# Wide matmuls on column groups for the feed-forward products and the shift vector, and folded modulation halves added on VectorE

## The chip, the cores and the metric

The kernel runs on one core of a Trainium2 chip. The metric is the device time of one execution in microseconds (us); the kernel before takes 594.23 us (median of three runs, 593.74 to 595.05). A core has five engines that follow their own instruction streams in order: PE (TensorE, matmuls; its weight loads are listed as PEld), DVE (VectorE), ACT (ScalarE), POOL (GpSimd) and SP (SyncE). Here POOL and SP do little but issue transfers (DMA), each into a queue of its own; 16 DMA engines carry both. SBUF is the on-chip memory of 128 partitions, PSUM the banks that matmuls write, DRAM the memory outside.

## What is computed

The reference is one transformer-like block, forward and backward, for a single token, in bfloat16. From a conditioning vector `c` it makes six vectors; shift, scale and gate for an attention part A, and shift, scale and gate for a feed-forward part B:

```python
mod = (_silu(c) @ w_mod).reshape(c.shape[0], 6, 1, -1)        # w_mod: 1024 x 6144
sa, ca, ga, sb, cb, gb = (mod[:, 0], ..., mod[:, 5])
h = _layernorm(x) * (1 + ca) + sa
x = x + ga * _A_ref(h, A_k_cache, A_v_cache, A_wq, A_wo)      # attention
h = _layernorm(x) * (1 + cb) + sb
x = x + gb * _B_ref(h, B_w_gate, B_w_up, B_w_down)            # sigmoid(h w_gate) * (h w_up), times w_down
```

A has 32 query heads of 128 and four key/value heads, and looks at the last 4096 of 65536 cached positions. B has 3584 hidden units. The outputs are the block's result and the gradients by every input: `x`, both caches (4 x 65536 x 128 each, zero outside the last 4096 positions), `wq`, `wo`, `w_gate`, `w_up`, `w_down`, `c` and `w_mod`. Weight gradients are outer products of two vectors, as large as the weights. The reference's own matmuls have one row, so all is bound by moving weights and gradients; the zeros of the two cache gradients alone are about 120 transfers of 1 MB.

## The kernel before

The order of the instructions on each engine is that of the source: the kernel is written under a manual schedule, so a position in the text is a position in the queue. Vectors of 1024 lie in columns: element `k*128 + p` on partition `p`, column `k`. A 1024x1024 weight is eight tiles of 128x1024 bf16.

A product of a vector with a weight is done in two ways. The *narrow* way (`mod_tiles`, `front`, `ffn_mm`) makes the weight the stationary operand and the vector column the moving one: one matmul gives one column of 128 results, already in column layout. The *wide* way (`rows_mm`, L432 to 438) makes the vector column, broadcast to 32 columns, the stationary operand and streams 32 columns of each of the weight's 128-column heads past it, in four column groups: group `a` writes partitions 32a to 32a+31. There every partition of a group holds the same row of results; `rows_to_cols` (L440 to 444) multiplies by `mask`, which is the identity repeated for the four groups, and sums 32 neighbours, on DVE, and so brings the row back into columns.

The work goes in stages, in the profile's times:

- 0 to 25 us: the tiles of the first two sections of `w_mod` (`wm01_t`) come in on SP's queue, loads of K, `wq` and V on POOL's. `mod_ps` is computed in the wide way (loop from L471), and the two sections of each tile are folded: the second half is multiplied by the broadcast layer norm `b1k` (`mulv`, L476, L489), and `w01_fold` (L453 to 469) transposes the sum of both halves into `w01_T`, as 16 matmuls with the identity into two fp32 banks, copied out by ACT ("A") or DVE ("V").
- 25 to 66: transposes of K and `wq`, queries, scores, softmax. At its end `rsum` (L590) is the reciprocal of the sums, and four zero fills wait for it on POOL.
- 68 to 155: products with V and the per-head work with `wo` (L709, `n_ps`).
- 155 to 305: `b_ps` (L766), 512 matmuls in units that other work is put between (`bch`); the other four sections of `w_mod` are loaded, multiplied and summed (`fold_sum`, L943). Here the shift vector `sb_` is made by `mod_tiles` (L384) in two halves, into `md_ps` (L954 to 983).
- 306 to 480: the feed-forward loop, seven blocks `q` of 512 hidden units. A block's tiles of `w_up` and `w_gate` come by `load_ug` (L936), `w_down` by `load_wd` (L924, SP). `front` (L1026) makes gate and up products, `gates` (L1037) the two sigmoids on ACT, `hh_ops` the hidden vector, `ffn_mm` (L1047) the product with `w_down`, which `ffn` sums over blocks. `wd_ttr` and `wd_outer` make the gradient of the hidden vector and of `w_down` (on DVE, lines 250 and 246), `dug_part` the gradient at gate and up, and the loop over `j` the gradient into `h2` and the outer products that are stored over the weights' tiles (`store_ug`, L942). `side()` puts in left-over transposes (L909, `tp_side`, copied by ACT at L910).
- 480 to 570: backward through attention. `op_ps` (L1160) rearranges the heads' outputs; then `dattn`, gradients of `wo`, V, `wq`, K and of the sections of `w_mod`.
- 570 to 592: only transfers.

Transfers of zeros are put at chosen places (`zero(n, after)`, lines 206, 200, 194, 191; in the feed-forward loop by the table `Z_FFN`), so that the queue always holds work. With `after`, or when a source tile isn't ready, POOL waits at its issue, and all that stands behind it on POOL waits too. PSUM banks come in rotation from `new_ps`, `new_tp` and `new_bank`/`new_acc`; the latter two share one bank, tag "acc", which `md_ps`, `fg` and `op_ps` use one after another.

Of the kernel before, what the change touches and what calls it, by code (L numbers as in the profile page):

```python
# [10 lines left out]
P = 128  # L11
# [48 lines left out]
def kernel(  # L60
# [157 lines left out]
    def new_ps(name="ps"):  # L218
        p, tag = next_pool()
        return p.tile([P, 512], FP32, name=name, tag=tag)  # L220
# [4 lines left out]
    def new_acc(name="acc"):  # L225
        return new_bank(name)[:, 0:64]
# [8 lines left out]
    def mulv(out, a, b):  # L235
        return tt(out, a, b, ALU.mult)

    def addv(out, a, b):
        return tt(out, a, b, ALU.add)

    def cp(out, a):
        return nc.vector.tensor_copy(out=out, in_=a)  # L242
# [138 lines left out]
        eng.dma_start(out=ar(off, 2 * n).rearrange("p (j x) -> p j x", j=n),  # L381
                            in_=wm_view[:, j:j + n, sct * D:(sct + 1) * D])

    def mod_tiles(ps, tiles, ts_, first, last=KD - 1):  # L384
        for t in ts_:
            for k in range(KD):
                nc.tensor.matmul(ps[:, k:k + 1], lhsT=tiles[t][:, k * P:(k + 1) * P],
                                 rhs=cs_bf[:, t:t + 1], start=(first and t == ts_[0] and k == 0), stop=(t == last),
                                 skip_group_check=True)

    def mod_rows(out, tiles):
        ps = new_bank("mod_rows")
# [45 lines left out]
        return mm  # L438

    def rows_to_cols(out, ps, n, room=scr):  # L440
        f = room.bitcast(FP32)[:, 0:32 * n].rearrange("p (n r) -> p n r", r=32)
        tt(f, ps[:, 0:32 * n].rearrange("p (n r) -> p n r", r=32),
           mask.rearrange("p (o r) -> p o r", o=1).broadcast_to([P, n, 32]), ALU.mult)
        nc.vector.reduce_sum(out=out, in_=f, axis=AX.X)
# [7 lines left out]

    def w01_fold(j, eng):  # L453
        cols = slice(j * P, (j + 1) * P)
        for k in range(2):
            ps = new_ps("w01_ps")
            for i in range(4):
                nb = 4 * k + i
                for sct in range(2):
                    c0 = sct * D + nb * P  # L460
                    nc.tensor.matmul(ps[:, i * P:(i + 1) * P], lhsT=wm01_t[j][:, c0:c0 + P], rhs=ident_bf[:, :],  # L461
                                     start=(i == 0 and sct == 0), stop=(sct == 1), skip_group_check=True)
            o = w01_T[:, 4 * k:4 * k + 4, cols]
            v = ps.rearrange("p (n m) -> p n m", n=4)
            if eng[k] == "A":
                nc.scalar.copy(out=o, in_=v)
            else:
                cp(o, v)

    rot[:] = [(psum, "mm"), (pna, "na"), (pgu, "gu"), (ppq, "pq"), (px, "x"), (pna, "na"), (prq, "rq")]  # L470
    mod_ps = new_bank("mod_ps")  # L471
    for j in range(KD):
        rows_mm(mod_ps, cs_bf[:, j:j + 1], heads(wm01_t[j]), j == 0, j == KD - 1)
        if j < KD - 1:
            mulv(wm01_t[j][:, D:2 * D], wm01_t[j][:, D:2 * D], b1k)
        if j > 1:  # L476
            w01_fold(j - 2, "AA")
    mod_col = vt([P, KM], "mod_col")
    rows_to_cols(mod_col[:, 0:16], mod_ps, 16)
    sa, ca, ga = mod_col[:, 0:8], mod_col[:, 8:16], mod_col[:, 16:24]  # L480
# [5 lines left out]
    addv(h1, h1, sa)  # L486
    h1_bf = vt([P, KD], "h1_bf", BF16)
    cp(h1_bf, h1)
    mulv(wm01_t[KD - 1][:, D:2 * D], wm01_t[KD - 1][:, D:2 * D], b1k)  # L489
    w01_fold(KD - 2, "AV")  # L490
    w01_fold(KD - 1, "AV")

    def kT_unit(i):
        g, tb = divmod(i, G)
# [456 lines left out]
    fold_T = [tr_unit(w2_t[t]) for t in range(KD)]  # L951

    h2 = vt([P, KD], "h2")
    md_ps = new_acc("md_ps")  # L954
    for t in range(4):
        fold_sum(t, (b1k, scr))
    bch(1)
    mod_tiles(md_ps, sb_t, range(4), True)
    bch(1)
    fold_T[0]()  # L960
    bch(1)
# [17 lines left out]
    wm_sec(5, 4, 1, 56, nc.sync)  # L979
    cp(scr, B_t[4])  # L980
    B_t[4] = scr
    mod_tiles(md_ps, sb_t, range(4, 8), False)
    cp(sb_, md_ps[:, 0:KD])
    mulv(h2, ln2, cb1)
    addv(h2, h2, sb_)
    h2_bf = vt([P, KD], "h2_bf", BF16)
# [1 line left out]
    for t in range(4, 8):  # L988
# [29 lines left out]
    small = [{k: vt([P, w], "%s%d" % (k, i), dt) for k, w, dt in  # L1018
              (("sg", 4, FP32), ("om", 4, FP32), ("dhh", 4, FP32), ("hh", 4, FP32), ("hh_bf", 4, BF16),
               ("hom", 4, FP32), ("dug_bf", 8, BF16))} for i in range(2)]  # L1020
    fg = new_acc("fg")
    ffn_ps = fg[:, 0:KD]
    ffn = vt([P, KD], "ffn")
    gu_t = [fg[:, 16 + 8 * i:24 + 8 * i] for i in range(2)]

    def front(q):  # L1026
        gu = gu_t[q % 2]
        for k in range(2):
            for j in range(KD):
                for i in range(4):  # L1030
                    f0 = 256 * (i // 2) + i % 2
                    col = 4 - 4 * k + i
                    nc.tensor.matmul(gu[:, col:col + 1], lhsT=ug_v[:, q % 2, j // 4, j % 4, k, f0:f0 + 255:2],  # L1033
                                     rhs=h2_bf[:, j:j + 1], start=(j == 0 and i == 0), stop=(j == KD - 1),
                                     skip_group_check=True)

    def gates(q):  # L1037
        r, gu = small[q % 2], gu_t[q % 2]
        nc.scalar.activation(out=r["sg"], in_=gu[:, 0:4], func=ACT.Sigmoid)
        nc.scalar.activation(out=r["om"], in_=gu[:, 0:4], func=ACT.Sigmoid, scale=-1.0)  # L1040

    def hh_ops(q):
        r, up = small[q % 2], gu_t[q % 2][:, 4:8]
        mulv(r["hh_bf"], r["sg"], up)
        mulv(r["hh"], r["sg"], up)
        mulv(r["hom"], r["hh"], r["om"])

    def ffn_mm(q, s):
        for i in (2 * s, 2 * s + 1):
            for k in range(KD):  # L1050
                nc.tensor.matmul(ffn_ps[:, k:k + 1], lhsT=wd_v[:, i, k * P:(k + 1) * P],  # L1051
                                 rhs=small[q % 2]["hh_bf"][:, i:i + 1], start=(i == 0 and k == 0),
                                 stop=(i == 3), skip_group_check=True)

    def wd_ttr(q, s):
        for i in (2 * s, 2 * s + 1):
# [42 lines left out]
    for q in range(NB):  # L1099
        z = Z_FFN[q]  # L1100
        more = q + 1 < NB
        for j in range(KD):
            w = ug_v[:, q % 2, j // 4, j % 4, :, :].rearrange("p k f -> p (k f)")
            ttr(w, w, dug_b, dh2acc[:, q * KD + j:q * KD + j + 1])
            if not more and j in (3, 5, 6):
                unpark({3: 2, 5: 0, 6: 4}[j])
            (outer_act if j < 5 else outer_dve)(w, h2[:, j:j + 1], dug_b)
            if more and j == 4:
                front(q + 1)
                gates(q + 1)  # L1110
            if more and (j > 4 or (j == 1 and q)):
                side()
            if j == 0:
                if q == 0:
                    cp(ffn, ffn_ps)
                else:
                    addv(ffn, ffn, ffn_ps)
            if j == 3:
                store_ug(q, 0, 4)
                zero(z[0])  # L1120
        store_ug(q, 4, 4)
        zero(z[1])
        if more:
            hh_ops(q + 1)
            ffn_mm(q + 1, 0)
            wd_ttr(q + 1, 0)
            wd_outer(q + 1, 0)
            ffn_mm(q + 1, 1)
            side(3 if q < 2 else 2)
            wd_ttr(q + 1, 1)  # L1130
            dug_part(q + 1)
            if q + 2 < NB:
                load_ug(q + 2, 0, 4)
            wd_outer(q + 1, 1)
            zero(z[2])
            side()
            if q + 2 < NB:
                load_ug(q + 2, 4, 4)
            zero(z[3])
            if q + 2 < NB:  # L1140
                load_wd(q + 2, 0)
                load_wd(q + 2, 1)
        else:
            zero(z[2] + z[3])
    assert not jobs
    for p in (1, 3):
        unpark(p)
    nc.scalar.copy(out=B_home[5], in_=B_t[5])
# [276 lines left out]
```

## Time and profile before

| | us |
|---|---|
| median of 3 runs | 594.23 (593.74 to 595.05) |
| profiled execution, its own time | 594.11 |
| its span | 592.3 |
| PE, PEld busy | 403.6, 256.7 |
| DVE, ACT, POOL busy | 364.3, 263.5, 156.4 |
| mean granted PE clock | 0.775 |
| bytes moved, mean rate | 246.57 MB, 416 GB/s |

The span runs from the first to the last recorded instruction or transfer of the profiled execution; its own time includes what lies around it. Busy times of different engines overlap. A row of a timeline or of the groups names the line, the engine, the operation, the tile that is written and read with its shape, and, in brackets, how long the engine was idle before it and which instruction ended that. Since most vector and copy work goes through helpers, several steps share a line: 233 is every elementwise product or sum of two tensors, 242 every copy on DVE, 246 a product with a per-partition scalar, 250 a product with a sum along the row, 436 every wide matmul. The tile names tell them apart; large tiles are views of one `arena`. The row of the granted clock gives 0.5 to 0.6 of full speed through most of the feed-forward loop.

### The profile page before, as it was taken

To read this page: it belongs to the slowest core of one execution; us is meant where nothing else is said; L and a number is where in the kernel's file an instruction comes from. 1 tells how busy PE (TensorE), PEld (TensorE's weight loads), DVE (VectorE), ACT (ScalarE), POOL (GpSimd) and SP (SyncE) were. 2 spreads that over 40 slices of the span, in tenths; PEclk is the share of its full clock that TensorE was granted. 3 is DMA by queue.
4 is the path that set the end of the run, shared out by engine and by line. 5 is a ranking of instruction groups with operands and counts; after the bars stand their busy time and mean duration, and the time that the engine had idled before them with its cause. 6 is when DMAs were issued, how large, how long until landed. Compare 5 with 4: busy or idle time off the path is not lost.

```text
span 592.3 us, 10137 instructions
## 1 busy us (share of the span) xinstructions
PE 403.6 (68%) x4107; PEld 256.7 (43%) x4132; DVE 364.3 (62%) x684; ACT 263.5 (44%) x401; POOL 156.4 (26%) x258
## 2 busy tenths in 40 slices
PE   3996689999999999978866236244363455977600
PEld 2784333334344546534436225244253335656500
DVE  3765499999511020176548686687866878778740
ACT  2589514567211014212135376464655645965400
POOL 3113123212223112222221334224343145113200
PEclk9999699999999999997995567555555558755555
DMA  8999999999999999999999999999999999999998
GB/s 349 420 420 420 413 454 392 464 421 430 425 422 397 432 452 419 433 431 400 413 422 395 419 413 413 411 411 416 415 414 413 418 419 408 416 426 420 414 419 360
DMA packets 37486, 246.57 MB, mean 416 GB/s; under 512 B 6097, under 2 KB 6097, under 8 KB 23712
## 3 DMA queue, kind: packets, MB, share of 16 engines
q0 software_dynamic: 30144, 218.65, 92.3%
q1 hardware_dynamic: 7248, 27.27, 12.7%
q8 instruction: 32, 0.52, 0.3%
q14 instruction: 14, 0.11, 0.1%
q10 hardware_dynamic: 48, 0.01, 0.0%
HBM read 78.28 MB, written 185.60 MB: 446 GB/s over the span
## 4 chain that ended last, share of the span: by engine, by line
PE 38%; DMA 23%; DVE 18%; issue 9%; ACT 6%; POOL 1%; ACTq 0%; DVEq 0%; POOLq 0%; SPq 0%
PE b_ps L766 17%; DMA out_dram<-arena 13%; DVE arena L233 6%; PE n_ps L709 6%; DMA arena<-in_B_w_down_dram 5%; DVE arena L250 5%; DMA arena<-in_B_w_gate_dram 4%; DVE arena L246 3%; ACT arena L519 2%; PE t_ps L667 2%; PE tp_side L909 1%; PE tp_k L498 1%; PE w_ps L461 1%; PE ok L629 1%; PE do L1189 1%
## 5 line engine op out<-in xcount | busy, mean ns | idle before, releaser
L766 PE MATMUL b_ps<-arena 128*128 128x512 bf16 x494 | 116.4, 384 | 2.5 <-ACT arena L910 1.1
L910 ACT COPY arena<-tp_side 128x1024 bf16<-128x1024 bf16 x62 | 60.9, 1015 | 71.2 <-PE tp_side L909 71.2
L233 DVE TENSOR_TENSOR arena<-arena 128x2048 bf16<-128x2048 bf16 x64 | 76.5, 1223 | 2.3 <-PE n_ps L709 0.3
L766 PEld LDWEIGHTS <-arena 128*128 128x128 bf16 x512 | 49.3, 99 | 59.0 <-issue 5.8
L250 DVE CUSTOM_DVE_ANT_0 arena<-arena,scr 128x1024 bf16<-128x1024 bf16 x56 | 66.2, 1221 | 9.3 <-ACT scr L1072 9.3
L709 PE MATMUL n_ps<-arena 128*128 128x512 bf16 x249 | 65.2, 378 | 6.2 <-DVE arena L233 4.2
L200 POOL DMA_DIRECT2D out_dram<-out_dram x68 | 33.6, 495 | 116.0 <-PE n_ps L709 37.5
L909 PE MATMUL tp_side<-ident_bf,arena 128*128 128x128 bf16 x496 | 53.9, 285 | 12.6 <-DVE arena L233 5.3
L909 PEld LDWEIGHTS <-arena 128*128 128x128 bf16 x496 | 46.0, 132 | 18.4 <-issue 9.8
L1033 PE MATMUL fg<-h_bf,arena 128*128 128x1 bf16 x448 | 15.6, 166 | 48.6 <-DMA arena<-in_B_w_up_dram 25.5
L709 PEld LDWEIGHTS <-arena 128*128 128x128 bf16 x256 | 24.6, 97 | 41.2 <-issue 15.8
L250 DVE CUSTOM_DVE_ANT_0 arena<-arena,b1k 128x1024 bf16<-128x1024 bf16 x24 | 28.4, 1221 | 20.5 <-PE fg L1051 20.5
L281 ACT ACTIVATE arena<-scr,h 128x1024 bf16<-128x1024 bf16 x35 | 38.5, 1143 | 2.7 <-DVE dh2acc L250 2.3
L206 POOL DMA_DIRECT2D out_dram<-zeros x45 | 25.1, 561 | 55.0 <-PE q_ps L436 14.0
L942 POOL DMA_DIRECT2D out_dram<-arena x28 | 22.1, 793 | 63.0 <-ACT arena L281 43.8
L1033 PEld LDWEIGHTS <-arena 128*128 128x128 bf16 x448 | 13.9, 104 | 51.2 <-DMA arena<-in_B_w_up_dram 31.2
L1253 ACT ACTIVATE arena<-ps_kv 128x512 bf16<-128x512 f32 x48 | 26.4, 618 | 21.6 <-PE ps_kv L1249 21.6
L669 ACT CAST arena<-t_ps 128x512 bf16<-128x512 f32 x56 | 30.1, 589 | 12.1 <-PE t_ps L667 12.1
L242 DVE CAST arena<-b_ps 128x512 bf16<-128x512 f32 x6 | 4.2, 692 | 50.8 <-PE b_ps L766 50.8
L1249 PE MATMUL ps_kv<-junk,arena 8*128 8x128 bf16 x256 | 28.7, 307 | 5.6 <-DVE arena L246 5.6
L1249 PEld LDWEIGHTS <-arena 8*128 8x128 bf16 x256 | 25.2, 141 | 9.9 <-issue 9.8
L519 ACT COPY arena<-tp_wq 128x1024 bf16<-128x1024 bf16 x23 | 21.4, 1070 | 7.3 <-PE tp_wq L517 7.3
(315 smaller groups left out, 634.3 us busy)
## 6 DMA issues: line engine op xcount, KB each, us to landing
out_dram<-zeros POOLq DMA_DIRECT2D x45, 1024.0 KB, 14.0
out_dram<-arena POOLq DMA_DIRECT2D x28, 1024.0 KB, 15.4
out_dram<-arena POOLq DMA_DIRECT2D x30, 512.0 KB, 11.5
out_dram<-arena SPq DMA_DIRECT2D x20, 512.0 KB, 10.4
arena<-in_A_wq_dram POOLq DMA_DIRECT2D x8, 1024.0 KB, 20.9
arena<-in_A_wo_dram POOLq DMA_DIRECT2D x8, 1024.0 KB, 12.4
arena<-in_w_mod_dram POOLq DMA_DIRECT2D x7, 1024.0 KB, 18.6
arena<-in_B_w_up_dram POOLq DMA_DIRECT2D x14, 512.0 KB, 12.0
```

What stands on the lines that cost most here:

```text
L200: ins = nc.gpsimd.dma_start(out=as_rows(region, BIGP).bitcast(FP32), in_=zero_src[:, 0:P * ZW // 4].rearrange("i (p x) -> (i p) x", p=BIGP ...
L233: return nc.vector.tensor_tensor(out=out, in0=a, in1=b, op=op)
L250: return nc.vector.tensor_tensor_reduce(out=out, in0=w, in1=b, scale=1.0, scalar=0.0, op0=ALU.mult, op1=ALU.add, accum_out=acc)
L281: return nc.scalar.activation(out=out, in_=b, func=ACT.Copy, scale=col)
L519: nc.scalar.copy(out=blk, in_=tp[:, :])
L669: nc.scalar.copy(out=o, in_=ps)
L709: mm = nc.tensor.matmul(nbank[k][:, :], lhsT=k_nat[:, g, t_ * DH:(t_ + 1) * DH], rhs=vp[:, t_ % 2, 4 * k:4 * k + 4, :].rearrange("p h d -> ...
L766: mm = nc.tensor.matmul(bbank[p][k][:, :], lhsT=a4[:, p, h, :], rhs=wo_t[u][:, a, k * 512:(k + 1) * 512], start=(i == 0 and a == 0), stop= ...
L909: nc.tensor.transpose(tp[:, i * P:(i + 1) * P], blk[:, i * P:(i + 1) * P], ident_bf[:, :])
L910: nc.scalar.copy(out=blk if dst is None else dst, in_=tp[:, :])
L1033: nc.tensor.matmul(gu[:, col:col + 1], lhsT=ug_v[:, q % 2, j // 4, j % 4, k, f0:f0 + 255:2], rhs=h2_bf[:, j:j + 1], start=(j == 0 and i == ...
L1249: nc.tensor.matmul(ps[:, t4 * DH:(t4 + 1) * DH], lhsT=rows[32 * g:32 * g + HG, t_ * P:(t_ + 1) * P], rhs=hd[32 * g:32 * g + HG, :], start= ...
```

## The change

Three products go from the narrow to the wide way: the shift vector, the gate and up products, and the product with `w_down`. In the feed-forward loop both share one PSUM bank, `fg`: 256 columns for gate and up, 256 for the result with `w_down`. Because parts of the bank are accumulated over different stretches, it is cleared by DVE and every matmul adds (`start=False`): once before the loop, and the gate and up part again after each `rows_to_cols`, which works in place in PSUM. The result of `w_down` is summed over all seven blocks in PSUM and brought into columns once, behind the loop, instead of one addition per block. `gates(q + 1)` is moved from the middle of the `j` loop to behind `store_ug` and `zero` at its end. The streamed operand of `front` reads every second element of the tile, as the narrow weight load did.

Separately, the two halves of a `wm01` tile are added on DVE (`addv`) after the product, and the fold is eight transposes into one bf16 tile and one copy, instead of 16 matmuls that add in PSUM and two copies.

No transfer is added, dropped or moved against the others of its queue.

```diff
-    def mod_tiles(ps, tiles, ts_, first, last=KD - 1):
+    def mod_tiles(ps, tiles, ts_):
         for t in ts_:
-            for k in range(KD):
-                nc.tensor.matmul(ps[:, k:k + 1], lhsT=tiles[t][:, k * P:(k + 1) * P],
-                                 rhs=cs_bf[:, t:t + 1], start=(first and t == ts_[0] and k == 0), stop=(t == last),
-                                 skip_group_check=True)
+            rows_mm(ps, cs_bf[:, t:t + 1], heads(tiles[t]), t == 0, t == KD - 1)
...
     def rows_to_cols(out, ps, n, room=scr):
-        f = room.bitcast(FP32)[:, 0:32 * n].rearrange("p (n r) -> p n r", r=32)
+        room = room if room is ps else room.bitcast(FP32)
+        f = room[:, 0:32 * n].rearrange("p (n r) -> p n r", r=32)
...
     def w01_fold(j, eng):
         cols = slice(j * P, (j + 1) * P)
-        for k in range(2):
-            ps = new_ps("w01_ps")
-            for i in range(4):
-                nb = 4 * k + i
-                for sct in range(2):
-                    c0 = sct * D + nb * P
-                    nc.tensor.matmul(ps[:, i * P:(i + 1) * P], lhsT=wm01_t[j][:, c0:c0 + P], rhs=ident_bf[:, :],
-                                     start=(i == 0 and sct == 0), stop=(sct == 1), skip_group_check=True)
...
+        tp = new_tp("tp_w01")
+        for nb in range(KD):
+            nc.tensor.transpose(tp[:, nb * P:(nb + 1) * P], wm01_t[j][:, nb * P:(nb + 1) * P], ident_bf[:, :])
...
+    def w01_sum(j):
+        w, v = wm01_t[j][:, 0:D], wm01_t[j][:, D:2 * D]
+        mulv(v, v, b1k)
+        addv(w, w, v)
...
         if j < KD - 1:
-            mulv(wm01_t[j][:, D:2 * D], wm01_t[j][:, D:2 * D], b1k)
+            w01_sum(j)
         if j > 1:
-            w01_fold(j - 2, "AA")
+            w01_fold(j - 2, "A")
...
-    mulv(wm01_t[KD - 1][:, D:2 * D], wm01_t[KD - 1][:, D:2 * D], b1k)
-    w01_fold(KD - 2, "AV")
-    w01_fold(KD - 1, "AV")
+    w01_sum(KD - 1)
+    w01_fold(KD - 2, "A")
+    w01_fold(KD - 1, "V")
...
-    md_ps = new_acc("md_ps")
+    md_ps = new_bank("md_ps")[:, 0:256]
...
-    cp(sb_, md_ps[:, 0:KD])
+    rows_to_cols(sb_, md_ps, KD, md_ps)
...
-    fg = new_acc("fg")
-    ffn_ps = fg[:, 0:KD]
+    fg = new_bank("fg")
+    nc.vector.memset(fg, 0.0)
+    gu_ps, ffn_ps = fg[:, 0:256], fg[:, 256:512]
     ffn = vt([P, KD], "ffn")
-    gu_t = [fg[:, 16 + 8 * i:24 + 8 * i] for i in range(2)]
+    gu_t = [gb_rest] * 2
+
+    def ffn_rows(out, col, w, stop):
+        for a in range(4):
+            nc.tensor.matmul(out[32 * a:32 * a + 32, :], lhsT=col.broadcast_to([P, 32]), rhs=w[..., 32 * a:32 * a + 32],
+                             start=False, stop=stop, tile_position=(0, 32 * a), skip_group_check=True)

     def front(q):
-        gu = gu_t[q % 2]
-        for k in range(2):
-            for j in range(KD):
-                for i in range(4):
-                    f0 = 256 * (i // 2) + i % 2
-                    col = 4 - 4 * k + i
-                    nc.tensor.matmul(gu[:, col:col + 1], lhsT=ug_v[:, q % 2, j // 4, j % 4, k, f0:f0 + 255:2],
-                                     rhs=h2_bf[:, j:j + 1], start=(j == 0 and i == 0), stop=(j == KD - 1),
-                                     skip_group_check=True)
+        for j in range(KD):
+            w = ug_v[:, q % 2, j // 4, j % 4, :, :].rearrange("p k (s r i) -> p (k s) i r", s=2, i=2)
+            ffn_rows(gu_ps, h2_bf[:, j:j + 1], w, j == KD - 1)

     def gates(q):
         r, gu = small[q % 2], gu_t[q % 2]
+        rows_to_cols(gu, gu_ps, 8, gu_ps)
+        nc.vector.memset(gu_ps, 0.0)
...
     def ffn_mm(q, s):
         for i in (2 * s, 2 * s + 1):
-            for k in range(KD):
-                nc.tensor.matmul(ffn_ps[:, k:k + 1], lhsT=wd_v[:, i, k * P:(k + 1) * P],
-                                 rhs=small[q % 2]["hh_bf"][:, i:i + 1], start=(i == 0 and k == 0),
-                                 stop=(i == 3), skip_group_check=True)
+            ffn_rows(ffn_ps, small[q % 2]["hh_bf"][:, i:i + 1], heads(wd_v[:, i, :]),
+                     q == NB - 1 and i == 3)
...
                 front(q + 1)
-                gates(q + 1)
             if more and (j > 4 or (j == 1 and q)):
                 side()
-            if j == 0:
-                if q == 0:
-                    cp(ffn, ffn_ps)
-                else:
-                    addv(ffn, ffn, ffn_ps)
...
         if more:
+            gates(q + 1)
             hh_ops(q + 1)
...
     assert not jobs
+    rows_to_cols(ffn, ffn_ps, KD, ffn_ps)
     for p in (1, 3):
         unpark(p)
```

## The prediction

> **What bounds the kernel now.** I read the head of the page first (busy time, slices), then windows at the edges of the span, then the timeline where the changed lines run, and last what POOL's queue waits for.
>
> The head of the page: engine, busy time, share of the span; then the slices.
>
> ```profile
> span 592.3 us, 10137 instructions
> PE 403.6 (68%) x4107; PEld 256.7 (43%) x4132; DVE 364.3 (62%) x684; ACT 263.5 (44%) x401; POOL 156.4 (26%) x258
> ...
> DMA  8999999999999999999999999999999999999998
> ...
> DMA packets 37486, 246.57 MB, mean 416 GB/s; under 512 B 6097, under 2 KB 6097, under 8 KB 23712
> ```
>
> No engine passes 68%, and the DMA engines are busy in every slice. The reader should see that the span is 246.57 MB at the rate of the transfers: 246.57 MB / 416 GB/s = 592.7 us. The windows (start:end, length, then per engine busy time and count, granted clock, DMA share, GB/s) say where the rate is not full:
>
> ```profile
> 0.00:2.00 2.00, 0.00 (x0) 0.00 (x0) 0.62 (x2) 0.00 (x0) 1.14 (x8) 1.00 0.20 21
> 2.00:4.00 2.00, 0.00 (x0) 0.00 (x0) 0.00 (x0) 1.28 (x1) 0.00 (x0) 1.00 0.75 290
> 4.00:10.00 6.00, 1.35 (x5) 1.10 (x5) 1.88 (x12) 1.70 (x3) 3.16 (x6) 1.00 1.03 418
> ...
> 330.00:340.00 10.00, 1.79 (x40) 1.71 (x41) 4.84 (x13) 0.38 (x1) 3.53 (x6) 0.50 1.07 417
> ...
> 570.00:580.00 10.00, 0.00 (x0) 0.00 (x0) 0.00 (x0) 0.00 (x0) 0.00 (x0) 0.50 1.02 419
> ```
>
> Only the first 4 us fall short; after 570 no engine computes, and 22 us of transfers are left. So work saved on PE shortens nothing by itself. Work added shortens nothing either, and costs only where it delays an instruction that issues transfers until the queues run dry: a dry microsecond is lost for good, since the bytes stay the same. I call "cover" the time from an issue on POOL to the landing of the last transfer issued before it. Three places matter: the zero fills after softmax, the stores inside the feed-forward loop, and the stores of the backward pass behind it. In POOL's timeline and its list of waits:
>
> ```profile
> 66.45 2.15 POOL L206 DMA_DIRECT2D out_dram<-zeros  x4 [7.69 <-DVE rsum L590]
> ```
> ```profile
> POOL out_dram L942 <- ACT arena L281: 43.8, 7, 8.4
> ...
> POOL out_dram L1258 <- ACT arena L1253: 15.8, 3, 10.8
> ```
>
> Each waits for computed data. Cover, from issue and landing times in the trace: at 66.45 the last earlier transfer (issued 58.02) lands 13.8 us on, at 71.8: 5.4 us. At 331.41 it is 7.9 (issue 327.26, 12.0 to land); at 405.41, 7.1 (401.83, 10.7); at 522.75, 8.9 (511.42, 20.2); at 528.42, 8.1. Not all cover can be spent: a new transfer needs a fixed time F before its bytes flow. Lower bound 2.5 us: the first load, issued at 0.74 on an empty queue, lands 3.8 us later, 1.25 of it for 512 KB at 418 GB/s. Upper bound 4.8: the load issued at 91.40 had 4.8 us of cover and no gap followed.
>
> **The change, part by part.** The run that was profiled took 594.11 us (span 592.3 and 1.8 around it); the median is 594.23, 0.12 above.
>
> *w01 fold.* Removed: eight of 16 matmuls per tile (16 took 1.07 us) and one of two fp32 copies (ACT 589 ns). Added: one sum on VectorE, 128x1024, 688 ns by the products of the same shape; in a row three such took 1.90, so about 0.65 each. Before, DVE was paced by PE, one tile per 1.33 us (15.74, 17.07, 18.40). Now it does 2 x 0.65 per tile itself, seven tiles from 13.06: to about 22.3, where `mod_ps` was read at 21.06: +1.3. The eighth pair stands behind h1, with its sum of 0.65 ahead of the last fold; that fold is half as long, and it saves one of the copies of 0.69. The first K transpose moves from 24.95 to about 26.6. Nothing between there and rsum is idle enough to absorb it (transposes and copies follow one another), so I take +1.7 at 66.45. Cover left 5.4 - 1.7 = 3.7: a gap of 0 (F=2.5) to 1.1 (F=4.8).
>
> *Shift vector.* 64 narrow matmuls (32 took 0.95) become 32 wide ones (0.99 for the same shape in `mod_rows`): PE -0.9. The copy (0.17) becomes product and reduction (0.42 + 0.42): +0.67 on DVE at 289. Its followers are fold sums; the queue there is 16 us deep. Nothing.
>
> *Entry of the loop.* A clearing of 128x512, between 0.3 and 0.5 by the 128x512 (0.48) and 128x128 (0.17) ones at the start. Gates gain rows_to_cols (0.84) and a clearing of 256 columns (about 0.3). With the shift of the start carried along, 1.7 + 0.4 + 1.2 = +3.3 at block 0. The stores of 331.41 then have 7.9 - 3.3 = 4.6 us: no gap, or 0.2 with F=4.8.
>
> *Front and gates in the loop.* Narrow, 64 matmuls take 1.81 us (28 ns each) at clock 0.50. The nearest wide row there is `do` (L1189): 64 of 512 columns in 5.76, 90 ns each; half of that for 256 is 45, and 32 make 1.44: PE -0.4, if reading every second element costs nothing; twice as long it is +1.1. The Trainium skill, "TensorE: Matmul & The Clock Gate", section "Back-to-back issue gap", gives one column per cycle of 1.2 GHz when the array is cold: 213 ns for 256 columns, by an estimate 1.7 us for eight rounds of four column groups at once. By it the front would save 0.1 instead of 0.4; neither moves the sum.
>
> What counts is order. `gates(q+1)` moves behind the last column of the block, so on ACT the sigmoids stand behind three `tp_side` copies, not ahead of them. Block 5 to 6 before (start, duration, engine, line, tile, idle before):
>
> ```profile
> 428.66 1.33 PE L1033 MATMUL fg<-h_bf,arena 128*128 128x1 bf16 x44 [2.01 <-DMA arena<-in_B_w_gate_dram]
> ...
> 430.02 0.17 ACT L1039 ACTIVATE sg<-fg 128x4 f32<-128x4 f32 x1 [5.16 <-PE fg L1033]
> ...
> 430.29 0.16 DVE L233 TENSOR_TENSOR hh_bf<-sg,fg 128x4 bf16<-128x4 f32 x1 [2.20 <-ACT om L1040]
> ...
> 430.90 1.93 ACT L910 COPY arena<-tp_side 128x1024 bf16<-128x1024 bf16 x2 [0.64 <-PE tp_side L909]
> ...
> 432.86 0.59 PE L1051 MATMUL fg<-hh_bf,arena 128*128 128x1 bf16 x16
> 433.01 1.01 ACT L910 COPY arena<-tp_side 128x1024 bf16<-128x1024 bf16 x1 [0.19 <-PE tp_side L909]
> 433.27 1.23 DVE L250 CUSTOM_DVE_ANT_0 arena<-arena,b1k 128x1024 bf16<-128x1024 bf16 x1 [2.55 <-PE fg L1051]
> ```
>
> After: sigmoids at 434.02, hh_bf at 434.3, the product with w_down at 434.6, the DVE pass that stood at 433.27 at about 435.3: +2.0. Rows_to_cols (0.84) fits into DVE's idle stretch ahead of 430.29. This happens where the front waits for its load (ends at 382.9, 430.0, 456.0). Where w_down comes later (335.87, 408.87) it hides it. The delay should not add up: each block starts anew at the landing of loads whose date the bytes ahead of them set. At 405.41, 2.0 to 3.3 off 7.1 leaves 3.8 to 5.1: gap 0 to 1.0. In each block 0.16 us (`ffn` sum) goes from DVE.
>
> *Behind the loop.* Last block +2.0, less 0.16, and rows_to_cols 0.84. `op_ps` (L1160, 1.45 us at 468.41, hidden before) shares the bank, so it starts after that; DVE's copy of it, at 478.01, now waits about 1.5. Queued behind it: the layer-norm gradient, `dattn`, the K/V gradients and their stores. Sum 2.0 - 0.16 + 0.84 + 1.5 = +4.1. The stores at 522 to 533 then have 4.0 to 4.8 us of cover: a gap of 0 to 0.8. The first dwo store (494.73) is not moved: its data is ready at about 487, and POOL is held by earlier landings.
>
> *Sum.* Ends: F=2.5 gives 0; F=4.8 gives 1.1 + 0.2 + 1.0 + 0.8 = +3.1. The nearest row for F on POOL's queue is its first transfer (issued 6.84, packets from 10.7: 3.9), nearer to the upper end; between it and 4.8 I take 4.4: 0.7 + 0 + 0.5 + 0.4 = +1.6. So 594.11 + 1.6, and 0.12 to the median: 595.8 us.
>
> By the Trainium skill, "DMA: Bandwidth & Descriptors", section "Anatomy of one DMA", the fixed part is about 2.0 us; as an estimate from that the sum would be 0 and the time 594.2. The first load's 2.5 is near it, but it ran alone, and 3.9 was measured on the queue that matters.
>
> **Rivals.** (0.2%, 1.2 us, is what a measurement of this kernel can tell from no change: 593.0 to 595.4 is "the same".)
>
> *Not slower: the cover holds.* All shifts fall into the queue, F is about 2.5, and the time stays 594.2 (593.2 to 595.2). For it: 22 us of transfers behind the last computation, 418 GB/s in every window from 4 us. It decides as long as cover minus shift stays above F at 66.45. Against it: 3.7 us is less than any cover seen without a gap. Chance 0.38.
>
> *Shifts add up in the loop.* If a later store delays the next load by as much, +2.0 per block over six blocks less the cover: 12 + 1.3 - (7.1 - 4.4) = +10 at worst; with half the blocks hidden, +4: 598 to 601. Against it: about 10 MB per block at 416 GB/s are 24 us, and the chain through stores and loads consists mostly of queueing. Chance 0.12.
>
> *Faster.* Eight hundred fewer matmuls and half the fold copies let the first stage end earlier, if DVE takes 0.5 per sum rather than 0.65, or transfers run at 418 throughout: 246.57 MB / 418 = 589.9, with 2.5 lost at the start 592.4, so 592.0 to 593.0. Nothing in the windows ties the rate to PE. Chance 0.12.
>
> My own forecast, gaps totalling +1.2 to +3.1, has 0.38, level with the first rival; I prefer it because all the shifts point one way.
>
> **How the numbers follow.** Slower 0.38 + 0.12 = 0.50, same 0.38, faster 0.12. Range 593.2 to 599.0: it leaves out most of faster (0.10) and half of the adding-up case (0.07). The forecast's own range is 595.4 to 597.3.
>
> **What would show it.** rsum near 68.1 instead of 66.45 and a dip of DMA share in 68 to 76; sigmoids behind the third side copy in each block; the copy of `op_ps` about 4 us later, and stores of 522 to 533 later by as much; DMA share below 0.9 in a window near 405 or 530. Wrong if the rates stay at 416 with all the shifts in place (the cover held), if rsum does not move, or if blocks take over 24.3 us each.

## The result, and the profile after

The changed kernel takes 596.14 us (median of 8 runs, 594.44 to 599.71); the kernel before, run beside it on the same chip, 594.47 (8 runs, 593.74 to 595.05). The ratio is 1.0035, 95% interval 1.0020 to 1.0051: slower by 1.2 to 3.0 us. Forecast were 595.8 us, 593.2 to 599.0, and slower as the likeliest sign. The spread is new: 5.3 us where the kernel before spreads over 1.3. The profile is of the longest of the eight, 599.71 us, so it shows more loss than the median has.

The head of the page of the changed kernel, answering to the lines shown of before:

```profile
span 597.9 us, 9287 instructions
PE 400.3 (67%) x3676; PEld 242.8 (41%) x3700; DVE 378.4 (63%) x709; ACT 262.8 (44%) x394; POOL 156.1 (26%) x258
...
DMA  8999999999999999999999999999999999989998
...
DMA packets 37484, 246.53 MB, mean 412 GB/s; under 512 B 6097, under 2 KB 6097, under 8 KB 23712
```

The kernel's own transfers move the same bytes (the instruction queue has 0.04 MB less); the rate is 412 GB/s and not 416: 246.53 MB / 412 are 598.4 us. PE does 3.3 us less, DVE 14.1 more, and neither is what the time follows. One digit of the DMA row fell. The windows (start:end, length, busy time and count per engine, granted clock, DMA share, GB/s) show where transfers went missing, at softmax's end, behind it and in the tail:

```profile
66.00:68.00 2.00, 1.50 (x13) 1.24 (x14) 0.23 (x1) 2.00 (x5) 0.00 (x0) 0.50 0.99 387
68.00:70.00 2.00, 1.81 (x17) 1.28 (x15) 0.19 (x2) 1.74 (x4) 0.00 (x0) 0.50 1.00 389
70.00:72.00 2.00, 1.37 (x10) 1.07 (x8) 0.69 (x3) 0.00 (x0) 1.57 (x3) 0.50 0.69 260
...
94.00:96.00 2.00, 1.79 (x15) 0.71 (x15) 1.97 (x4) 0.00 (x0) 1.29 (x2) 1.00 0.25 98
96.00:98.00 2.00, 1.37 (x6) 0.57 (x6) 2.00 (x3) 0.00 (x0) 0.02 (x1) 1.00 0.79 147
98.00:100.00 2.00, 2.00 (x11) 0.88 (x9) 1.95 (x2) 1.07 (x2) 1.02 (x2) 1.00 1.76 723
...
530.00:532.00 2.00, 2.00 (x22) 0.90 (x21) 1.34 (x3) 1.19 (x2) 0.00 (x0) 0.50 0.93 393
532.00:534.00 2.00, 2.00 (x25) 2.00 (x20) 2.00 (x4) 1.70 (x4) 0.53 (x1) 0.50 0.25 94
534.00:536.00 2.00, 1.27 (x12) 1.00 (x10) 2.00 (x3) 2.00 (x5) 0.83 (x1) 0.50 0.93 369
```

The rates between 88 and 110 us need care. A window counts all bytes of a packet where the packet starts, and here packets of 64 KB, which take about 2.4 us each in the trace, stand among small ones; a DMA share of 1.76 says as much. With each packet's bytes spread over its time, the three windows from 94 us have 428, 179 and 402 GB/s: the dry stretch is that of 96 to 98 alone.

The first and the last of the three are places that the prediction named. But the first comes from more than the work that was added. `rsum` (L588) stands at 69.97 us instead of 66.00: 4.0 us late, where 1.7 was predicted. PE's timeline, of the kernel before (two lines) and of the changed kernel (three), shows the rest:

```profile
23.94 1.01 PE L461 MATMUL w_ps<-ident_bf,arena 128*128 128x128 bf16 x15 [0.98 <-DVE arena L233]
24.79 4.63 PE L498 MATMUL tp_k<-ident_bf,arena 128*128 128x128 bf16 x80
...
22.24 0.62 PE L455 MATMUL tp_w<-ident_bf,arena 128*128 128x128 bf16 x8 [0.71 <-DVE arena L233]
25.70 1.03 PE L455 MATMUL tp_w<-ident_bf,arena 128*128 128x128 bf16 x8 [2.83 <-DVE arena L233]
26.52 6.86 PE L496 MATMUL tp_k<-ident_bf,arena 128*128 128x128 bf16 x80
```

The eight transposes before the idle stretch of 2.83 us take 0.62 us, the same eight behind it 1.03, and the 80 transposes of K take 6.86 us where they took 4.63 before. The windows, first one of the kernel before and then those of the changed kernel, have the reason in the column of the granted clock, the third from the right:

```profile
24.00:26.00 2.00, 2.00 (x37) 2.00 (x38) 1.50 (x3) 0.59 (x1) 0.53 (x1) 1.00 1.00 418
...
24.00:26.00 2.00, 0.30 (x4) 0.31 (x5) 1.57 (x4) 0.00 (x0) 0.18 (x1) 0.59 1.01 410
26.00:28.00 2.00, 2.00 (x21) 2.00 (x20) 1.07 (x2) 0.00 (x0) 0.53 (x1) 0.50 1.01 422
28.00:30.00 2.00, 2.00 (x22) 2.00 (x20) 1.68 (x3) 0.00 (x0) 0.19 (x1) 0.50 1.02 426
30.00:32.00 2.00, 2.00 (x29) 2.00 (x27) 1.68 (x4) 0.00 (x0) 0.34 (x1) 0.70 1.00 418
```

Before, the clock was 1.00 in every window from 20 to 36 us; there the longest idle stretch at this place was 0.98 us. The Trainium skill, "TensorE: Matmul & The Clock Gate", section "What's actually happening", says that the clock halves after an idle window of about 3.4 us, and that the window runs freely, so that the moment differs between executions of one kernel. The halving and the difference agree with the traces here; that 2.83 us between matmuls were enough, after several shorter idle stretches, shows that the nominal window is no safe limit.

### The profile page after: what moved, and what is told of

It is laid out like the page before. It is cut to its first block, busy times and chain, and to the rows that moved or that the text cites. A ratio compares the mean times of both kernels' runs of the same rounds, so it can differ in the third digit from the quotient of the medians.

```text
span 597.9 us, 9287 instructions
## 1 busy us (share of the span) xinstructions
PE 400.3 (67%) x3676; PEld 242.8 (41%) x3700; DVE 378.4 (63%) x709; ACT 262.8 (44%) x394; POOL 156.1 (26%) x258
## 2 busy tenths in 40 slices
DMA packets 37484, 246.53 MB, mean 412 GB/s; under 512 B 6097, under 2 KB 6097, under 8 KB 23712
## 4 chain that ended last, share of the span: by engine, by line
PE 38%; DVE 20%; DMA 18%; issue 11%; ACT 7%; POOL 2%; ACTq 0%; DVEq 0%; POOLq 0%; SPq 0%
PE b_ps L764 16%; DMA out_dram<-arena 8%; DVE arena L233 7%; DMA arena<-in_B_w_gate_dram 6%; PE n_ps L707 6%; DVE arena L250 4%; DVE arena L246 3%; DMA arena<-in_B_w_down_dram 3%; ACT arena L517 2%; PE t_ps L665 2%; PE tp_side L907 2%; PE tp_k L496 2%; ACT arena L908 1%; PE do L1183 1%; PE fg L1027 1%
## 5 line engine op out<-in xcount | busy, mean ns | idle before, releaser
L233 DVE TENSOR_TENSOR arena<-arena 128x2048 bf16<-128x2048 bf16 (+1 forms) x72 | 82.0, 1164 | 2.6 <-PE n_ps L707 0.3
L764 PEld LDWEIGHTS <-arena 128*128 128x128 bf16 x512 | 49.2, 99 | 59.1 <-issue 5.7
L907 PE MATMUL tp_side<-ident_bf,arena 128*128 128x128 bf16 x496 | 52.0, 278 | 15.4 <-ACT arena L908 6.4
L907 PEld LDWEIGHTS <-arena 128*128 128x128 bf16 x496 | 44.1, 129 | 25.5 <-issue 15.9
L1027 PE MATMUL fg<-arena,h_bf 128*32 128x256 bf16 x224 | 14.2, 411 | 44.5 <-DMA arena<-in_B_w_gate_dram 44.5
L707 PEld LDWEIGHTS <-arena 128*128 128x128 bf16 x256 | 24.6, 97 | 41.3 <-issue 15.8
L1027 PEld LDWEIGHTS <-h_bf 128*32 128x32 bf16 x224 | 6.8, 128 | 50.1 <-DMA arena<-in_B_w_gate_dram 41.2
```

The lines of the kernel that those rows point to most:

```text
L233: return nc.vector.tensor_tensor(out=out, in0=a, in1=b, op=op)
L707: mm = nc.tensor.matmul(nbank[k][:, :], lhsT=k_nat[:, g, t_ * DH:(t_ + 1) * DH], rhs=vp[:, t_ % 2, 4 * k:4 * k + 4, :].rearrange("p h d -> ...
L764: mm = nc.tensor.matmul(bbank[p][k][:, :], lhsT=a4[:, p, h, :], rhs=wo_t[u][:, a, k * 512:(k + 1) * 512], start=(i == 0 and a == 0), stop= ...
L907: nc.tensor.transpose(tp[:, i * P:(i + 1) * P], blk[:, i * P:(i + 1) * P], ident_bf[:, :])
L1027: nc.tensor.matmul(out[32 * a:32 * a + 32, :], lhsT=col.broadcast_to([P, 32]), rhs=w[..., 32 * a:32 * a + 32], start=False, stop=stop, til ...
```

## The experiments

Times are medians beside the kernel before on the same chip, whose median was 594.17 to 594.30 in these comparisons. My theory after reading the traces: the first stage comes late because DVE has more to do and because PE, idling meanwhile, loses its clock; then the queue runs dry. Rivals: the feed-forward part and the tail make the loss; or something that is not in the moved work.

**The changed kernel once more** (no edit).

> The changed kernel once more, unchanged. Its profiled execution took 599.71 us, its median 596.14. Theory (the queue runs dry where computed data come late): rsum again near 70 us instead of 66, the copy of op_ps again about 6 us later than before, time 595.5 to 597. Rival (the profiled execution is long because TensorE waited for its instructions, 1.8 us in tp_P and 2.8 us in mv_dcs, and not because of the moved work): without these two waits the transfers of the tail have no gap, and the time of that execution is within 1 us of 594.5.

Measured 595.58 us, ratio 1.0028 (1.0016 to 1.0040). The profiled execution was a short one, 594.51 us. Here the clock was low for less time:

```profile
26.55 5.66 PE L496 MATMUL tp_k<-ident_bf,arena 128*128 128x128 bf16 x80
```

`rsum` was at 68.8, 2.8 us late, and the 64 matmuls behind it (L627), for which the kernel before takes 5.95 us, took 3.64 at a better clock: by the second load of wo (95.68 before, 95.97 here) the delay was down to 0.3 us. So the delay itself differs from execution to execution, as the times do. The waits of TensorE that the page puts down to "issue" were missing, and so was the loss in the tail; the rival on them is half right, since in this execution both are gone together.

**The w01 part alone**, on the kernel before.

```diff
         if j < KD - 1:
-            mulv(wm01_t[j][:, D:2 * D], wm01_t[j][:, D:2 * D], b1k)
+            w01_sum(j)
         if j > 1:
-            w01_fold(j - 2, "AA")
+            w01_fold(j - 2, "A")
...
```

> The kernel before with the w01 part alone (sum on VectorE, eight transposes and one copy). Theory: TensorE idles for about 2.8 us before the last fold and the granted clock falls, so the first 80 K transposes take 6.9 us instead of 4.6; rsum 3.5 to 4 us late, transfers thin out between 64 and 72 us, and the time grows by 0.5 to 1.3 us (594.9 to 595.8). Rival (the start costs nothing, all of the loss is in the feed-forward part and behind it): rsum late as well, time as before, 594.2 to 594.7.

Measured 596.15 us, ratio 1.0033 (1.0020 to 1.0047): the whole loss. K transposes 6.81 us, `rsum` at 69.9, and this thin stretch:

```profile
68.00:70.00 2.00, 1.81 (x16) 1.28 (x15) 0.25 (x2) 1.68 (x4) 0.00 (x0) 0.50 1.01 385
70.00:72.00 2.00, 1.30 (x10) 1.01 (x7) 0.70 (x3) 0.00 (x0) 1.63 (x4) 0.50 0.60 223
```

It lost 0.4 us more than the bound I had set.

**All but the w01 part**: the changed kernel with `w01_fold` as before.

```diff
-            w01_sum(j)
+            mulv(wm01_t[j][:, D:2 * D], wm01_t[j][:, D:2 * D], b1k)
...
-            w01_fold(j - 2, "A")
+            w01_fold(j - 2, "AA")
...
```

> The changed kernel with the w01 part undone. Theory: start as before (rsum at 66.0), the copy of op_ps still 5 to 6 us late, transfers thin between 500 and 540 us; time 594.9 to 596.0. Rival (the start makes the whole difference): 594.2 to 594.7. Rival (the delay of the start travels through to the tail): the copy of op_ps 2 to 3 us late instead of 6.

Measured 594.31 us, ratio 1.0002 (0.9994 to 1.0011). My expectation missed: the wide matmuls, the moved gates and the product behind the loop cost nothing that can be measured. They do shift the work, and in the order foreseen; the sigmoids stand behind the third copy (ACT's timeline of this kernel), where they were at 430.02 before:

```profile
430.50 1.93 ACT L908 COPY arena<-tp_side 128x1024 bf16<-128x1024 bf16 x2 [5.61 <-PE tp_side L907]
432.62 1.01 ACT L908 COPY arena<-tp_side 128x1024 bf16<-128x1024 bf16 x1 [0.18 <-PE tp_side L907]
433.52 0.21 ACT L1039 ACTIVATE sg<-gb_rest 128x4 f32<-128x4 f32 x1
```

and the copy of `op_ps` comes 3.0 us later (481.01 for 478.01). The rate from 320 to 420 us is 415 GB/s all the same. So the expectation's first rival holds: the start makes the difference.

**PE kept busy**: the changed kernel with twelve matmuls between the last two folds, whose result nothing reads.

```diff
     w01_fold(KD - 2, "A")
+    idle = new_ps("idle")
+    for _ in range(12):
+        nc.tensor.matmul(idle[:, :], lhsT=ident_bf[:, :], rhs=wm01_t[0][:, 0:512], start=True, stop=True)
     w01_fold(KD - 1, "V")
```

> The changed kernel with twelve matmuls of 512 columns into a spare bank between the last two folds, where TensorE idles for 2.8 us; nothing reads their result. Theory (the granted clock fell because of that idle stretch): K transposes back at 4.6 to 4.9 us for 80, rsum near 67.8 instead of 70, no thin stretch at 70 to 72 us, time 0.5 to 1.2 us below the changed kernel. Rival (the K transposes are slow for another reason, the copies on VectorE or their order): 80 K transposes still near 6.9 us, rsum at 70 or later, time as the changed kernel.

Measured 594.54 us, ratio 1.0009 (0.9999 to 1.0019). PE's timeline of this kernel:

```profile
22.68 2.75 PE L491 MATMUL idle<-arena,ident_bf 128*128 128x512 bf16 x12
25.68 0.62 PE L455 MATMUL tp_w<-ident_bf,arena 128*128 128x128 bf16 x8 [0.25 <-DVE arena L233]
26.13 4.63 PE L499 MATMUL tp_k<-ident_bf,arena 128*128 128x128 bf16 x80
```

The fold starts where it did (25.68 for 25.70), so the added DVE work is still there; only PE was busy ahead of it, and K transposes are back at 4.63 us, `rsum` at 67.3. That shows the cause of the slow transposes: the idle stretch, not the copies. Of the 1.3 us that the changed kernel lost in the same comparison (again), 1.0 are gone with useless work on PE. Nine of the twelve runs lie between 593.9 and 594.8; three, the profiled one among them, between 596.7 and 597.3, which nothing I varied explains.

**Useful work in its place**: the last fold behind the first five K transposes, its copy on ACT.

```diff
     w01_fold(KD - 2, "A")
-    w01_fold(KD - 1, "V")
...
     for i in range(10):
         kT_unit(i)
+        if i == 4:
+            w01_fold(KD - 1, "A")
```

> The changed kernel with the last fold put behind the first five K transposes, and its copy on ACT, so that TensorE has work while the last sum is made. Theory: no idle stretch of 2.8 us, clock stays at 1.0 between 20 and 40 us, first 80 K transposes done by about 31 us, rsum at 66 to 66.8; no thin stretch at 70; time 594.0 to 594.7, like the kernel before. Rival (the w01 part costs by its work on VectorE, not by the idle TensorE): rsum 67.3 or later, time 595 or more.

Measured 594.13 us, ratio 1.0002 (0.9993 to 1.0011); `rsum` at 65.8, 0.2 us before that of the kernel before. The same kernel once more:

> The k_first kernel once more, to see how often it falls as high as 595.2: median 594.0 to 594.4. Theory: with TensorE kept busy its first stage is that of the kernel before in every execution, so the spread is that of the kernel before, about 1 us. Rival (the start's clock still differs from execution to execution): a spread of 2 us or more, as in the changed kernel.

594.41 us, ratio 1.0004 (0.9996 to 1.0013), spread 1.6 us. So the whole change can be had at the old time with one line moved. It does not beat the kernel before.

**What lateness at rsum costs by itself**: the kernel before, clock untouched, with three or seven needless reductions ahead of `rsum`.

```diff
+    for _ in range(3):
+        nc.vector.reduce_sum(out=ssum4, in_=ident_f.rearrange("p (o r) -> p o r", o=1).broadcast_to([P, 4, P]), axis=AX.X)
     rsum = vt([P, 1], "rsum")
```

> The kernel before with three needless reductions on VectorE ahead of rsum, about 2 us, whose result nothing reads; TensorE's clock in the first 60 us is untouched. Theory: cover at the wait is 5.4 us, and F, the time a new transfer needs before its bytes flow, about 2.8 by the thin stretch of the w01 run; 2 us late leaves 3.4, more than F, so no loss: 594.1 to 594.6. Rival (F is 4.4, as predicted): loss 1.0, time 595.0 to 595.6.

> The kernel before with seven needless reductions ahead of rsum, about 4.8 us. Theory (F about 2.8): cover left 0.6, loss about 2.2 us, time 596.0 to 597.0. Rival (F is 4.4): loss 3.8, 597.6 to 598.5. Rival (lateness at rsum alone costs nothing, the clock or something else in the w01 part does): 594.1 to 594.7.

`rsum` came 2.9 and 6.0 us late (68.9, 72.0). The reductions make 2.1 and 4.9 of it, about as meant; 0.8 and 1.0 stood already at the K transposes (25.59 and 25.82 for 24.79); these two profiled executions reached the full clock at 17.16 and 17.43 us, that of the kernel before at 14.94. The 80 transposes took 4.63 us in both, as before. Times 595.34 us, ratio 1.0023 (1.0015 to 1.0032), and 599.31, ratio 1.0080 (1.0067 to 1.0093): +1.2 and +5.1, both above what I had expected. So lateness alone costs, without slow K transposes. The windows of the kernel before (three lines) and of the second, late5:

```profile
68.00:70.00 2.00, 1.76 (x20) 0.69 (x24) 2.00 (x6) 1.78 (x9) 0.61 (x2) 0.50 1.06 403
70.00:72.00 2.00, 2.00 (x24) 0.71 (x20) 1.58 (x2) 1.50 (x8) 0.00 (x0) 0.50 1.15 436
72.00:74.00 2.00, 2.00 (x32) 0.76 (x24) 0.00 (x0) 0.00 (x0) 0.00 (x0) 0.76 1.15 426
...
68.00:70.00 2.00, 0.00 (x0) 0.00 (x0) 1.90 (x4) 0.00 (x0) 0.00 (x0) 0.50 0.88 334
70.00:72.00 2.00, 0.00 (x0) 0.00 (x0) 1.93 (x4) 0.00 (x0) 0.00 (x0) 0.50 0.22 88
72.00:74.00 2.00, 0.88 (x6) 0.62 (x10) 1.02 (x5) 0.14 (x1) 1.58 (x3) 0.50 0.34 131
```

Against 403, 436 and 426 GB/s before, 69 + 348 + 295 GB/s are missing in three windows of 2 us: at 425, 3.4 us. With 5.4 us of cover and 6.0 late, F is 3.4 - 0.6 = 2.8 us here; the first of the two runs, late2, with 344 and 397 GB/s from 68 to 72, gives (59 + 39) x 2 / 425 = 0.5 us at 2.9 late, F = 3.0. But that is not all that was lost: 5.1 is 1.7 more than 3.4. The rest is made at another place.

**Covering the waits**: the four zero fills at `nbias`, some 5 us before `rsum`; the load of wo behind the next fill; both; and both in the kernel before.

```diff
-    ts(nbias, mx, -SCALE, ALU.mult)
+    zero(Z_SM, ts(nbias, mx, -SCALE, ALU.mult))
...
-    zero(Z_SM, last)
...
                 gb_cols = mod_gb((6, 7))
-                load_wo(0)
...
+            if s == 28:
+                load_wo(0)
```

> The changed kernel with the four zero fills that waited for rsum tied to nbias instead, some 5 us earlier on VectorE; their bytes and their place in the queue stay. Theory (the loss of the first stage is made at this one wait, where the queue runs dry): the idle TensorE, the low clock and the late rsum stay as they are, the thin stretch at 68 to 72 us is gone, time 594.2 to 594.8. Rival (the late start costs by moving all that follows): the thin stretch appears later, time stays 595.5 to 596.5.

> The changed kernel with the load of wo's first tile moved behind the next zero fill, and the zero fills left at rsum. Theory of two dry places: 0.5 to 1.2 us still lost at 68 to 72, nothing at 93 to 97; time 594.6 to 595.3. Rival (only the first place counts): as the changed kernel, 595.5 to 596.5. Rival (only the second counts): 594.0 to 594.5.

> The changed kernel with the four zero fills tied to nbias (as in zeros_early) and, besides, the load of wo's first tile moved behind the next zero fill on POOL (from unit 24 to unit 28 of the stage with n_ps), where it waits for g_ps. Theory (the queue runs dry at two places that the late start reaches, 68 to 72 and 93 to 97 us; covering the first alone only moved the loss to the second): both thin stretches gone with rsum still 3 to 4 us late, time 594.0 to 594.6. Rival (a late start costs wherever the next thin place is, whatever is covered): 595.2 to 596.5.

> The kernel before with both moves of transfers (zero fills at nbias, the load of wo's first tile behind the next fill). Theory: the kernel before already thins out at 94 to 96 us (234 GB/s); covered, it gains 0.3 to 0.7 us: 593.5 to 593.9. Rival (that dip is made up for by faster stretches on both sides and costs nothing): 594.0 to 594.4.

| kernel | us | ratio (95%) |
|---|---|---|
| fills at nbias (zeros_early) | 596.44 | 1.0039 (1.0025 to 1.0053) |
| load moved (swap) | 595.93 | 1.0031 (1.0018 to 1.0044) |
| both (cover) | 596.40 | 1.0034 (1.0022 to 1.0046) |
| both, kernel before (before_cover) | 594.29 | 0.9999 (0.9991 to 1.0008) |

With the fills moved up, the thin stretch at 68 to 72 us is gone (397 and 434 GB/s) and the time stays. The windows of zeros_early have it later:

```profile
94.00:96.00 2.00, 1.27 (x7) 0.50 (x6) 2.00 (x3) 0.00 (x0) 0.83 (x2) 1.00 0.37 78
96.00:98.00 2.00, 1.89 (x10) 0.78 (x9) 2.00 (x3) 0.26 (x1) 0.21 (x1) 1.00 0.96 317
```

and with the load moved as well it is later still; the window of cover:

```profile
100.00:102.00 2.00, 2.00 (x11) 0.94 (x10) 1.86 (x3) 1.57 (x4) 1.78 (x3) 1.00 0.92 283
```

With the bytes spread over their packets' time, the two windows of zeros_early have 241 and 316 GB/s and that of cover 274.

My theory of two places, each to be covered by itself, falls; its rival, that lateness costs wherever the next thin place is, stands. Turning the order of issues round adds no bytes ahead of the end of the stage's first group (the second load of wo, 95.68 before), and that, by my reading, is what counts. From the sizes and end times of the transfers in each trace I took how much later than the kernel before a kernel has moved the same bytes, at 110 us of the kernel before, and set it beside the lateness of that second load:

| kernel | K transposes, us | rsum late | second load of wo late | bytes late at 110 | at 520 | at 590 |
|---|---|---|---|---|---|---|
| no_w01 | 4.63 | -0.3 | -0.2 | -0.2 | -0.4 | -0.6 |
| again | 5.66 | 2.8 | 0.3 | 0.3 | 0.2 | 0.2 |
| swap | 5.64 | 2.8 | 0.2 | 0.1 | 0.1 | 1.9 |
| fill | 4.63 | 1.3 | 1.5 | 0.5 | 1.5 | 3.2 |
| zeros_early | 6.26 | 2.8 | 2.1 | 1.2 | 1.0 | 1.4 |
| late2 | 4.63 | 2.9 | 2.4 | 1.3 | 1.2 | 1.2 |
| w01_only | 6.81 | 3.9 | 3.2 | 2.2 | 2.1 | 2.1 |
| changed | 6.86 | 4.0 | 3.3 | 2.5 | 2.3 | 5.7 |
| cover | 7.00 | 4.1 | 3.5 | 1.6 | 2.0 | 1.7 |
| late5 | 4.63 | 6.0 | 5.8 | 4.7 | 4.6 | 4.6 |

Beyond about 1 us, each microsecond by which that load is late is a microsecond of transfers lost (2.1 to 1.2, 3.2 to 2.2, 5.8 to 4.7; cover, with 3.5 to 1.6, loses somewhat less), and in most of these executions the loss stays nearly the same from there to 520 us: the feed-forward loop neither makes it worse nor gives it back (fill, which lost 1.1 us near 335, is the exception). Moving bytes from a later stage to before that place would be the test of this relation; it wasn't tried.

## Why the prediction was right, and where it was not

*Slower, through gaps in the queue where an issue waits for late data:* right, and shown by late2 and late5, which add nothing but lateness. The sum of +1.6 is met by 1.7 (596.14 - 594.47), but by other terms: that the two agree so closely is luck.

*w01 fold, +1.7 at rsum, a gap of 0.7:* the step that was mis-sized. The added DVE work was as worked out: `mod_ps` is read at 22.10, 1.04 us later (1.3 predicted), the K transposes start at 26.52 (26.6 predicted). What the step left out is the clock: PE stands idle 2.83 us and then, over six profiled executions, runs the 80 transposes in 5.64 to 7.00 us for 4.63, so `rsum` is 2.8 to 4.1 us late. The fill and k_first runs show this. The sentence that nothing between there and `rsum` could absorb the delay was true; that nothing could add to it was assumed and not said.

*F, between 2.5 and 4.8, 4.4 taken:* at `rsum` F is 2.8 to 3.0, near the lower end. The figure of the Trainium skill that was cited ("DMA: Bandwidth & Descriptors", section "Anatomy of one DMA", about 2.0 us) is nearer to this than my 4.4. Nor is F here what it was called, a time before the new transfer's bytes flow: in late5 the first packet of the zero fills starts at 73.55 us, 1.1 us after the issue at 72.42, while the bytes of the load ahead thin out from 69.5, 2.3 us before its landing. The upper bound holds. In windows of 2 us the kernel before seems to have a gap behind the load at 91.40:

```profile
92.00:94.00 2.00, 1.27 (x7) 0.48 (x5) 2.00 (x3) 0.00 (x0) 0.71 (x2) 1.00 0.79 330
94.00:96.00 2.00, 1.89 (x10) 0.78 (x8) 2.00 (x3) 0.37 (x1) 0.32 (x1) 1.00 0.66 234
96.00:98.00 2.00, 2.00 (x11) 0.88 (x9) 1.87 (x2) 1.79 (x4) 2.00 (x4) 1.00 1.58 645
```

but that is the counting of the 64 KB packets again: spread over their time, the bytes of these windows make 430, 410 and 401 GB/s. That fits before_cover, which puts the next zero fill ahead of this load and gains nothing, where I had expected 0.3 to 0.7 us.

*The load at 91.40, used as a bound only:* the step that was missed. It is the place with the least cover that I had found, 4.8 us, and the lateness of the start was not carried to it: 4.8 - 1.7 = 3.1, with F at 4.4 a gap of up to 1.3 that the sum lacks. In fill, late2, zeros_early, late5, w01_only and the changed kernel the cover at this load is 2.6 to 3.2 us, and 0.7 to 1.4 us of transfers are lost between 90 and 110. Cover and loss together make F 3.7 to 4.4 there: F is not the same at every issue, and at this one it is about what was taken.

*Shift vector, entry of the loop, gates behind the side copies, +2.0 per block, no adding up:* right in kind. In no_w01 the first DVE pass with w_down comes at 434.44, 1.2 us later than 433.27, and no delay adds up. The gap of 0.5 given for 405 us is not there: the bytes are never more than 0.3 us late in no_w01 from 310 to 560. The rival on adding up, at 0.12, falls. The front itself saves nothing when it runs in one piece: 32 wide matmuls take 1.90 us (at 325.67, clock 0.50), 64 narrow ones took 1.81, where -0.4 was predicted; no time hangs on it.

*Behind the loop, +4.1 and a gap of 0.4:* the copy of `op_ps` is 3.0 us later in no_w01, and without loss. In the profiled execution of the changed kernel it is 6.2 us late, and 3.4 us more are lost between 520 and 590 (the last two columns), about 2.2 of them from 530 to 538. Why in this execution and not in again or cover is not settled; the next section but one has what was seen.

*Not slower (0.38):* that is what the change without w01 does, and what all of it does once PE has work. The condition given, cover minus shift above F at 66.45, was failed by the shift, not by F.

*Faster (0.12):* no kernel with the change is; the lowest medians, 594.13 (k_first) and 594.31 (no_w01), are level with the kernel before, 594.17 and 594.25.

## What to carry to other kernels

Where transfers bound the time, carry every delay to each issue that has little cover behind it, and to the one with the least first. Look for dry stretches in short windows, but see how the bytes are counted: where packets take longer than a window, a rate of 234 GB/s beside one of 645 need be no gap at all, and a DMA share well above 1 gives it away. When work moves from PE to another engine, ask what PE does meanwhile: an idle stretch of under 3 us cost 1.0 to 2.4 us through the clock on the transposes that followed, beside 1.7 for the added work itself, and one fold put behind work that was ready took the cost away.

## What was not expected of the hardware

*The clock makes part of the spread.* The kernel before spreads over 1.3 us or less, the changed one over 3 to 5, and its two profiled executions differ at one place first: 80 K transposes in 6.86 or 5.66 us, then 64 matmuls in 5.28 or 3.64. In the traces the granted clock changes at distances that are multiples of 3.41 us, from another starting point in each execution. In the six executions with the idle stretch it fell after a step of 3.41 us in which PE was busy for 0.62 to 1.24 us; it stayed low after steps with 1.98 to 2.38 and rose after steps with 2.92 or more. So the low clock lasted 6.83 us in the changed kernel (24.37 to 31.20) and 3.41 in again (25.30 to 28.71). It isn't all of the spread: fill, whose clock stays full there, still spreads over 3.4 us.

*TensorE waiting for nothing that the profile names.* PE's timeline of the changed kernel in the tail:

```profile
511.81 1.32 PE L1222 MATMUL tp_P<-ident_bf,pT 128*32 128x128 bf16 x60
514.95 1.13 PE L1222 MATMUL tp_P<-ident_bf,pT 128*32 128x128 bf16 x68 [1.82 <-issue]
516.02 1.59 PE L337 MATMUL bc_ps<-ident_bf,dq_bf 128*128 128x128 bf16 x24
518.14 0.87 PE L337 MATMUL bc_ps<-ident_bf,dq_bf 128*128 128x128 bf16 x8 [0.53 <-ACT arena L1224]
518.85 0.84 PE L270 MATMUL mv_dcs<-dh_hl,arena 128*128 128x2 bf16 x28
522.52 1.10 PE L270 MATMUL mv_dcs<-dh_hl,arena 128*128 128x2 bf16 x36 [2.83 <-issue]
```

Between the two breaks lie 68 + 24 + 8 + 28 = 128 matmuls, each with a weight load: 256 instructions. In w01_only the breaks are at other matmuls (52 + 32 + 44), again 128 apart. The page's instruction queue moves 0.48 MB in 29 transfers, 16 KB each, and has one within a few microseconds of each break. The Trainium skill, "Runtime: NRT & Kernel Launch", section "Instruction fetch mechanics", says that an engine's program comes in blocks of 16 KiB, 256 instructions, by DMA, and that the cost of crossing one is mostly hidden; the distance of the breaks agrees, and hidden it was not here, with 1.8 and 2.8 us, while the queues were full. That these waits were for code is argued, not shown: no run moved the block boundaries alone, and again, with the same code, has none of them. Nor do they decide the time alone: w01_only has 1.9, 1.5 and 1.1 us of them and no loss after 520 us, swap has 2.2 and 0.9 and loses 1.7 there.
